# Transposes in visits of eight, two sub-blocks' transposes on VectorE, and the last output rows by two engines

## The chip, the cores and the metric

One core of a Trainium2 chip. The metric is the device time of one execution in microseconds. The kernel before takes 866.93 us in the median of three runs (866.83 to 867.17).

## What is computed

Three stages, one after the other, on 2304 tokens of width 512:

```python
scores = scale * np.matmul(q, k.transpose(0, 1, 3, 2))   # 4 batches, 8 heads, 576 tokens, 64 wide
mask = (rel >= 0) & (rel < 64)                           # a window of 64 tokens
attn = softmax(np.where(mask, scores, -1e9)); x = np.matmul(attn, v)
h = x @ w_in; x = np.maximum(h, 0) ** 2 @ w_out          # 512 -> 2048 -> 512
h = x @ w2_in; P = a0 + a1*h + a2*h2 + a3*h3
Q = 1 + abs(b0)*abs(h) + abs(b1)*h2; out = (P / (Q + 1e-6)) @ w2_out
```

Inputs and output are float32. Each large product is made of three float32r matmuls on high and low parts (high x high, high x low, low x high).

## The kernel before

The tokens are cut into five blocks of 512 (the last has 256), and into 18 sub-blocks of 128, numbered from 0. Attention is done by sub-block. Layer 1 (`l` = 0, the squared ReLU) runs over the blocks in order, layer 2 (`l` = 1, the rational function) after it over the blocks with the last two swapped. Within a block the 2048 hidden columns go by in 16 steps `j` of 128: `h_mm` (lines 776 to 803; matmuls on L788, L798) makes the hidden columns, `mid1` or `mid2` (L869, L911) applies the function and splits the result into high and low parts, and `out_mm` (L809; matmuls on L819 for layer 1, L821 for layer 2) adds the product into the four accumulators in PSUM. While block b of layer 1 runs, the attention of block b + 1 is done in slots that lie between its matmuls (`slots_of`, L969), and the weights are read and split on the way by `convert` (L422): in block 0 those of layer 1, needed at once (last operation L458, tiles `wih`, `wil`, `wo`), in blocks 1 to 3 those of layer 2, which go back to DRAM.

A sub-block `i` has these slots. `slot_q` and `slot_k` (L503, L522) turn its queries and keys: four TensorE transposes each (L515, L538) into a PSUM bank, then a copy by ScalarE or VectorE. From sub-block `NPE` = 10 on they are not turned on TensorE: `squares` (L351) copies queries and keys within DRAM, in pieces of 32 floats, into an order from which VectorE's transpose of 32 x 32 squares (L507, L529) does the rest. The scores (`slot_s`, matmuls on L621) go into two banks; `softmax` (L630) follows on VectorE and ScalarE. `slot_p` (L688) turns the probabilities, twice per sub-block, by four TensorE transposes (L699) and a copy (L704); from sub-block `NPD` = 8 on they are written to DRAM and read back in four pieces by POOL's DMA queue (L684, L685) and turned by VectorE (L692). `slot_x` (L728) makes the values (L708) and `split_x` their high and low parts. For sub-blocks after the block's first and below NPD, `slot_sx` puts the scores of `i` and the values of `i - 1` into one visit of TensorE. Outside the first block the PSUM banks for transposes and scores are `t0` and `t1`.

The order of the work is found when the kernel is built. `Plan.add` (L58) collects items, each with the engines that could do it, a cost in ns, the buffers that it reads and writes and a due time; `Plan.run` (L91) takes again and again the item that can start first, the more urgent of equals, and so fixes each engine's order, and that of SP's DMA queue ("dma"). The hardware then follows that order with semaphores. Slots are spread over 0.9 of a block's planned span (L1020 to L1024). The squares copies are listed from L1004 on: the item of step 9 + 2c + y (c the pair of heads, y keys or queries) of batch 2, and 17 + 2c + y of batch 3, each waiting for that step's low part from `mid1`. One item is four DMAs of SP.

The last block of layer 2 ends with accumulator 3. Its last matmuls are split into two halves of 256 columns (L826 to L833), and `evac2` (L946) copies each half out (L956) and stores it by SP (L957); all other rows are copied and stored whole (L962, L963).

```python
179      NPE = sum(n for _, n in blocks[:2]) // 128 + 2
...
973      o += ([("sx", i)] if first < i < NPD else [("s", i), ("x", i - 1)] if i > first else [("s", i)])
...
1008     sq_list.append((9 + 2 * c + y if z < B - 1 else 17 + 2 * c + y, x, c, z))
```

Of the kernel before, what the change touches and what calls it, by code (L numbers as in the profile page):

```python
# [47 lines left out]
class Plan:  # L48
# [9 lines left out]
    def add(self, engines, emit, reads=(), writes=(), due=None):  # L58
        it = Item(engines, emit, due)
        for b in reads:  # L60
            assert b.writers and not b.over
            for w in b.writers:
                it.deps[w] = True
        for b in writes:
            assert not b.over
            if not b.writers:
                for p in b.prev:
                    for w in p.writers + p.readers:
                        it.deps[w] = True
            for w in b.writers + b.readers:  # L70
                it.deps[w] = True
        for b in reads:
            b.readers.append(it)
        for b in writes:
            b.writers.append(it)
        it.deps.pop(it, None)
        for d in it.deps:
            d.users.append(it)
        self.items.append(it)
        return it  # L80

# [63 lines left out]
def window_attention__moe_relu2__moe_rational_kernel(  # L145
# [355 lines left out]
    qT, kT, sm, pT = {}, {}, {}, {}  # L501

    def slot_q(i, due):  # L503
        src = nat["q", i]
        if i >= NPE:
            t = qT[i] = buf(QTP, [128, HP, 128])
            plan.add({"dve": dve(512)}, lambda e: V.transpose(  # L507
                t.t.rearrange("p c t -> p (c t)"), src.t.rearrange("p h d -> p (h d)")), [src], [t], due)
            return
        ps = ps_buf()  # L510

        def tr(_):
            s = src.t.rearrange("p h d -> p (h d)")
            for c in range(HP):
                T.transpose(ps.t[:, c, :], s[:, c * 128:(c + 1) * 128], ident)  # L515

        plan.add({"pe": 430}, tr, [src], [ps], due).slack = rest(i)
        t = qT[i] = buf(QTP, [128, HP, 128])
        plan.add({"act": act(512, True), "dve": dve(512)}, lambda e: (
            A.copy(out=t.t, in_=ps.t) if e == "act" else V.tensor_copy(t.t, ps.t)), [ps], [t])  # L520

    def slot_k(i, due):  # L522
# [16 lines left out]

        plan.add({"pe": 430}, tr, [src], [ps], due).slack = rest(i)  # L540
        if i < NS0:
# [146 lines left out]
    def slot_p(i, n, due):  # L688
# [11 lines left out]

        plan.add({"pe": 430}, tr, [src] + [f for _, f in [own[i]] if n] if i in own else [src], [ps], due).slack = rest(i)
        t = pT[i, n] = early(NF - 5 - i, 2 + n, 128) if i < NS0 else buf(PT, [128, 4, 128])
# [53 lines left out]
    def split_x(i, ps):  # L756
# [3 lines left out]
        if bi == 0 and 2 * o == blocks[0][1]:  # L760
# [8 lines left out]

    fns = {"y": slot_y, "K": lambda z, due: slot_half("k", z, due), "Q": lambda z, due: slot_half("q", z, due),  # L770
           "S": slot_S, "q": slot_q, "k": slot_k, "s": slot_s, "sx": slot_sx, "p": slot_p, "x": slot_x}


# [32 lines left out]

    ends = []

    def out_mm(l, bi, j, g, due):  # L809
        n = blocks[bi][1]  # L810
        gh, gl = g
        wh, wl = wt[l, j, 1]

        def mm(m, cs=slice(0, KT)):
            for z, (w, y) in enumerate(((wh, gh), (wh, gl), (wl, gh)) if l == 0 else
                                       ((wh, gh), (wl, gh), (wh, gl))):
                st, en = (j == 0 and z == 0), (j == NF - 1 and z == 2 and cs.stop == KT)
                if l == 0:
                    T.matmul(out=v4(acc[l, bi, m].t, n), lhsT=w.t[:, m, :], rhs=y.t[:, :n // 128, :], start=st, stop=en)  # L819
                else:  # L820
                    T.matmul(out=v4(acc[l, bi, m].t, DM)[:, cs], lhsT=y.t[:, m, :], rhs=w.t[:, cs], start=st, stop=en)  # L821

        for m in range(KT if l == 0 else n // 128):
            if j == 0:
                acc[l, bi, m] = buf(f"acc{m}", [128, 512], F32, psum)
            if l and bi == orders[1][-1]:  # L826
                if j == NF - 1 and m == n // 128 - 1:
                    ends.extend(halves(acc[l, bi, m]))
                    for z, b in enumerate(ends):
                        b.prev = []  # L830
                        plan.add({"pe": 3 * MM[256]}, lambda e, m=m, z=z: mm(m, slice(2 * z, 2 * z + 2)),
                                 [wh, wl, gh, gl, acc[l, bi, m]], [b], due + z)
                    continue  # L833
            plan.add({"pe": 3 * MM[n if l == 0 else 512]}, lambda e, m=m: mm(m), [wh, wl, gh, gl], [acc[l, bi, m]],
                     due + m)
# [110 lines left out]
    def evac2(bi):  # L946
        t0, n = blocks[bi]
        for m in range(n // 128):
            due = finish - (n // 128 - 1 - m) * 1400 if bi == orders[1][-1] else finish
            if due == finish and ends:  # L950
                c = acc[1, bi, m]
                for z, b in enumerate(ends):
                    o = buf(LD, [128, H, D], view=lambda t: t.rearrange("p h d -> p (h d)")[:, 0:256])
                    cs = slice(z * 256, z * 256 + 256)
                    plan.add({"act": act(256, True), "dve": dve(256)}, lambda e, cs=cs, o=o: (
                        A.copy(out=o.t, in_=c.t[:, cs]) if e == "act" else V.tensor_copy(o.t, c.t[:, cs])), [b], [o])  # L956
                    plan.add({"dma": 364}, lambda e, o=o, m=m, cs=cs: nc.sync.dma_start(  # L957
                        out=out[t0 + m * 128:t0 + (m + 1) * 128, cs], in_=o.t), [o], due=due)
                continue
            c, o = acc[1, bi, m], buf(LD, [128, H, D], view=lambda t: t.rearrange("p h d -> p (h d)"))  # L960
            plan.add({"act": act(DM, True), "dve": dve(DM)}, lambda e, c=c, o=o: (
                A.copy(out=o.t, in_=c.t) if e == "act" else V.tensor_copy(o.t, c.t)), [c], [o])  # L962
            plan.add({"dma": 728}, lambda e, o=o, m=m: nc.sync.dma_start(  # L963
                out=out[t0 + m * 128:t0 + (m + 1) * 128, :], in_=o.t), [o], due=due)

# [3 lines left out]
    def slots_of(first, last):  # L969

        o = []
        for i in range(first, last):
# [121 lines left out]
```

## Time and profile before

| what | value |
|---|---|
| median of three runs | 866.93 us (866.83 to 867.17) |
| the profiled execution: its time, its span | 866.46 us, 864.5 us |
| TensorE matmuls (PE) | 856.6 us busy, 99% of the span |
| weight loads (PEld) | 717.2 us, 83% |
| VectorE (DVE) | 644.1 us, 74% |
| ScalarE (ACT) | 548.4 us, 63% |
| GpSimd (POOL) | 66.6 us, 8% |
| granted TensorE clock | 1.00, which is 2.4 GHz |

The span is what the profiler saw of the program; the rest of the execution's own time, 2.0 us, lies around it. Busy times are shares of the whole span, while the stages have different limits: layer 1 with the attention beside it goes on to about 380 us, layer 2 follows. Matmuls are pipelined: one begins before the last has ended, so the times that count are those from start to start. In the timelines, several like instructions that follow one another stand as one line, with their count at its end.

### The profile page before, as it was taken

How to read it: one execution, taken by the hardware profiler on the slowest of the kernel's cores; microseconds unless marked ns; L12 is line 12 of the kernel's file. 1: busy time of each engine (PE TensorE's matmuls, PEld its weight loads, DVE VectorE, ACT ScalarE, POOL GpSimd, SP SyncE). 2: the span in 40 equal slices, each digit the busy share in tenths (PEclk: the TensorE clock that was granted, in tenths of full speed). 3: DMA queues.
4: the chain of work that ended last, by engine and by line, in shares of the span. 5: the costliest groups of instructions: out<-in, count | busy, mean ns of one | idle time of the engine just before them, and what ended most of it. 6: DMA issues, size and time to landing. Idle time of an engine off the chain costs nothing.

```text
span 864.5 us, 14326 instructions
## 1 busy us (share of the span) xinstructions
PE 856.6 (99%) x5195; PEld 717.2 (83%) x5195; DVE 644.1 (74%) x1388; ACT 548.4 (63%) x1153; POOL 66.6 (8%) x124
## 2 busy tenths in 40 slices
PE   8999999999999999999999999999999999999998
PEld 7888888888888888888999888888888888988886
DVE  6999855666576656444313999999999999989994
ACT  7888755556554555554445766666666666878773
POOL 3000002222022221120000000000000000000000
PEclk9999999999999999999999999999999999999999
DMA  9977966999587776643499900300020003000001
GB/s 192 277 226 226 240 142 171 277 256 292 162 291 218 215 239 216 223 146 122 174 329 328 314 1 2 132 15 0 1 80 19 0 1 122 26 1 25 0 1 50
DMA packets 159831, 124.29 MB, mean 144 GB/s; under 512 B 94864, under 2 KB 136080, under 8 KB 157712
## 3 DMA queue, kind: packets, MB, share of 16 engines
q1 hardware_dynamic: 155600, 112.88, 44.5%
q0 software_dynamic: 4160, 10.49, 4.1%
q8 instruction: 41, 0.67, 0.3%
q14 instruction: 30, 0.25, 0.1%
HBM read 87.17 MB, written 40.37 MB: 148 GB/s over the span
## 4 chain that ended last, share of the span: by engine, by line
PE 98%; DVE 2%; ACT 0%; issue 0%; POOL 0%; ACTq 0%; POOLq 0%; DVEq 0%
PE h L798 34%; PE acc L819 23%; PE acc L821 23%; PE t L798 11%; PE t L621 2%; PE t L708 1%; PE t L699 0%; PE h L708 0%; DVE wih L655 0%; PE acc L984 0%; PE t L515 0%; PE acc L708 0%; DVE wil L655 0%; PE t L627 0%; PE h L788 0%; DVE wo L704 0%
## 5 line engine op out<-in xcount | busy, mean ns | idle before, releaser
L819 PE MATMUL acc<-g,wo 128*128 128x512 f32 (+1 forms) x960 | 214.5, 371 | 0.0
L819 PEld LDWEIGHTS acc<-g,wo 128*128 128x128 f32 x960 | 167.1, 189 | 30.6 <-issue 0.5
L798 PE MATMUL h<-xh,wih 128*128 128x512 f32 (+1 forms) x476 | 177.4, 373 | 0.0
L798 PE MATMUL h<-xl,wih 128*128 128x512 f32 (+1 forms) x476 | 175.3, 368 | 0.0
L798 PE MATMUL h<-xh,wil 128*128 128x512 f32 (+1 forms) x476 | 175.2, 368 | 0.0
L881 DVE TENSOR_TENSOR g<-cvr,g 128x512 fp32r<-128x512 f32 (+1 forms) x80 | 50.8, 635 | 98.5 <-ACT cvr L879 98.4
L874 ACT ACTIVATE cvr<-h 128x512 f32<-128x512 f32 (+1 forms) x80 | 44.2, 553 | 113.6 <-PE h L798 108.7
L798 PEld LDWEIGHTS h<-xh,wih 128*128 128x128 f32 x476 | 89.7, 189 | 16.0 <-issue 1.2
L798 PEld LDWEIGHTS h<-xh,wil 128*128 128x128 f32 x476 | 89.8, 189 | 15.2
L798 PEld LDWEIGHTS h<-xl,wih 128*128 128x128 f32 x476 | 89.8, 189 | 14.3
L821 PE MATMUL acc<-wo,cvr 128*128 128x512 f32 (+1 forms) x387 | 93.6, 388 | 0.0
L821 PE MATMUL acc<-wo,g 128*128 128x512 f32 x384 | 93.1, 390 | 0.0
L821 PEld LDWEIGHTS acc<-wo,cvr 128*128 128x128 f32 x387 | 71.8, 188 | 14.4
L821 PEld LDWEIGHTS acc<-wo,g 128*128 128x128 f32 x384 | 71.6, 188 | 14.5
L925 DVE SCALAR_TENSOR_TENSOR kT<-kT,b,sm 128x512 f32<-128x512 f32 (+1 forms) x80 | 55.7, 696 | 16.1 <-ACT kT L920 13.3
L927 ACT ACTIVATE raw<-kT,cb 128x512 f32<-128x512 f32 (+1 forms) x80 | 54.9, 686 | 8.8 <-DVE kT L925 5.5
L798 PE MATMUL t<-xl,wih 128*128 128x512 f32 (+1 forms) x160 | 58.9, 368 | 0.0
L798 PE MATMUL t<-xh,wil 128*128 128x512 f32 (+1 forms) x160 | 58.9, 368 | 0.0
L798 PE MATMUL t<-xh,wih 128*128 128x512 f32 (+1 forms) x160 | 58.8, 368 | 0.0
L659 ACT ACTIVATE sm<-sm,nm 128x128 f32<-128x128 f32 x112 | 43.8, 393 | 22.3 <-DVE nm L655 22.0
L938 DVE SCALAR_TENSOR_TENSOR pT<-pT,coef,raw 128x512 f32<-128x512 f32 (+1 forms) x80 | 55.7, 696 | 1.7
L921 ACT ACTIVATE sm<-h,coef 128x512 f32<-128x512 f32 (+1 forms) x40 | 25.8, 646 | 47.5 <-PE h L798 47.5
(176 smaller groups left out, 1356.5 us busy)
## 6 DMA issues: line engine op xcount, KB each, us to landing
raw<-in_moe_w_in_dram SPq DMA_DIRECT2D x60, 256.0 KB, 4.2
raw<-in_moe_w_out_dram SPq DMA_DIRECT2D x30, 512.0 KB, 4.6
w2h_d<-raw SPq DMA_DIRECT2D x32, 256.0 KB, 3.5
w2l_d<-cvr SPq DMA_DIRECT2D x32, 256.0 KB, 3.7
ld<-in_v_dram SPq DMA_DIRECT2D x25, 256.0 KB, 4.5
p_d<-sm POOLq DMA_DIRECT2D x20, 256.0 KB, 3.9
sm<-p_d POOLq DMA_DIRECT2D x80, 64.0 KB, 4.6
out_dram<-ld SPq DMA_DIRECT2D x17, 256.0 KB, 2.1
```

The source lines that it names most:

```text
L621: T.matmul(out=ps[gl].t[o:o + 64, hp, :], lhsT=qt.t[r, hp, gl * W:(gl + 1) * W], rhs=kt.t[r, hp, -W - 128:][:, :128] if not gl else kt.t[r ...
L659: A.activation(out=head(c), in_=head(c), func=ACTF.Exp, scale=-1.0, bias=nm.t[:, c:c + 1], accum_out=su.t[:, c:c + 1])
L708: T.matmul(out=ps.t[e * 64:(e + 1) * 64, hp, gl * W:(gl + 1) * W], lhsT=v.t[rows, 2 * hp + e, :], rhs=(pT[i, gl].t[:, (e ^ gl) * 2:(e ^ gl ...
L798: T.matmul(out=v4(hp.t, n), lhsT=w.t[:, (c ^ 2) * 128:((c ^ 2) + 1) * 128], rhs=x.t[:, :n // 128, c, :], start=(c == 0 and z == 0), stop=( ...
L819: T.matmul(out=v4(acc[l, bi, m].t, n), lhsT=w.t[:, m, :], rhs=y.t[:, :n // 128, :], start=st, stop=en)
L821: T.matmul(out=v4(acc[l, bi, m].t, DM)[:, cs], lhsT=y.t[:, m, :], rhs=w.t[:, cs], start=st, stop=en)
L874: plan.add({"act": act(n, True)}, lambda e: A.activation(out=r.t[:, :n], in_=hp.t[:, :n], func=ACTF.Relu), [hp], [r])
L881: plan.add({"dve": dve(n)}, lambda e: V.tensor_tensor(out=gl.t[:, :nq], in0=v4(r.t, n), in1=gh.t[:, :nq].bitcast(F32), op=ALU.subtract), [ ...
L921: plan.add({"act": act(n, True, 1)}, lambda e: A.activation(out=f(ab), in_=f(hb), func=ACTF.Abs, scale=coef[:, 4:5]), [hb, coef_b], [ab])
L925: plan.add({"dve": dve(n, ptr=1)}, lambda e: V.scalar_tensor_tensor(out=f(h2), in0=f(h2), scalar=b1, in1=f(ab), op0=ALU.mult, op1=ALU.add) ...
L927: plan.add({"act": act(n, ptr=1)}, lambda e: A.activation(out=f(y), in_=f(h2), func=ACTF.Ln, scale=2.0 ** -63, bias=cb[:, 0:1]), [h2], [y])
L938: plan.add({"dve": dve(n, ptr=1)}, lambda e: V.scalar_tensor_tensor(out=f(u), in0=f(u), scalar=coef[:, 0:1], in1=f(y), op0=ALU.subtract, o ...
```

## The change

The constants become NPE = 9 and NPD = 7: sub-block 9's queries and keys and sub-block 7's probabilities are turned by VectorE. The squares of batch 2 are copied five steps earlier. In the slots, `paired` joins a sub-block's query and key transposes into one item of TensorE with eight transposes, and likewise its two probability transposes; the joined item stands where the query's slot stood, or the second probability's. In the blocks concerned these are queries and keys of sub-blocks 6, 7 and 8 and probabilities of 5 and 6. The last matmuls are no longer split; the two halves of the last 128 rows are copied by ScalarE and VectorE, and stored by ScalarE's and SP's queues.

```diff
-    NPE = sum(n for _, n in blocks[:2]) // 128 + 2
-    NPD = sum(n for _, n in blocks[:2]) // 128
+    NPE = sum(n for _, n in blocks[:2]) // 128 + 1
+    NPD = sum(n for _, n in blocks[:2]) // 128 - 1
...
+    joint = []
+
+    def visit(reads, ps, tr, due, i):
+
+        if joint and joint[0]:
+            it, fs = joint.pop()
+            fs.append(tr)
+            plan.link(it, reads, [ps])
+            return
+        fs = [tr]
+        it = plan.add({"pe": 860 if joint else 430}, lambda e: [f(e) for f in fs], reads, [ps], due)
+        it.slack = rest(i)
+        if joint:
+            joint[0] = it, fs
+
+    def slot_qk(i, due):
+        joint.append(None)
+        slot_q(i, due)
+        slot_k(i, due)
+
+    def slot_pp(i, due):
+        joint.append(None)
+        slot_p(i, 0, due)
+        slot_p(i, 1, due)
...
-        plan.add({"pe": 430}, tr, [src], [ps], due).slack = rest(i)
+        visit([src], ps, tr, due, i)
...
-        def mm(m, cs=slice(0, KT)):
+        def mm(m):
...
-            if l and bi == orders[1][-1]:
-                if j == NF - 1 and m == n // 128 - 1:
-                    ends.extend(halves(acc[l, bi, m]))
...
+            if bi == orders[1][-1] and due == finish:
+                for z, e in enumerate(("act", "dve")):
+                    cs = slice(z * DM // 2, (z + 1) * DM // 2)
+                    o = buf(LD, [128, H, D], view=lambda t: t.rearrange("p h d -> p (h d)")[:, :DM // 2])
+                    plan.add({e: 334}, lambda e, o=o, c=c, cs=cs: (
+                        A.copy(out=o.t, in_=c.t[:, cs]) if e == "act" else V.tensor_copy(o.t, c.t[:, cs])), [c], [o])
+                    plan.add({"dma": 364}, lambda _, o=o, e=e, cs=cs, rows=rows: (A if e == "act" else nc.sync).dma_start(
+                        out=rows[:, cs], in_=o.t), [o], due=due)
                 continue
...
+    def paired(slots, first):
+
+        o = []
+        for x, d in slots:
+            kind, i = x[:2]
+            if kind in "qk" and first < i < NPE:
+                o += [(("qk", i), d)] if kind == "q" else []
+            elif kind == "p" and first <= i < NPD:
+                o += [(("pp", i), d)] if x[2] else []
+            else:
+                o.append((x, d))
+        return o
...
-                sq_list.append((9 + 2 * c + y if z < B - 1 else 17 + 2 * c + y, x, c, z))
+                sq_list.append((4 + 2 * c + y if z < B - 1 else 17 + 2 * c + y, x, c, z))
...
-                    slots = [(x, start[0, bi] + per * y) for y, x in enumerate(slots)]
+                    slots = paired([(x, start[0, bi] + per * y) for y, x in enumerate(slots)], f + 1)
```

## Rows read from the trace of the kernel before

**Rows 1.** The page's chain that ended last, shares of the span by engine.

```profile
PE 98%; DVE 2%; ACT 0%; issue 0%; POOL 0%; ACTq 0%; POOLq 0%; DVEq 0%
```

**Rows 2.** Windows: busy us of each engine (instructions), clock, DMA share, GB/s.

```profile
core 0: us, PE busy (x) PEld busy (x) DVE busy (x) ACT busy (x) POOL busy (x), PEclk, DMA share, GB/s
...
60.00:93.00 33.00, 33.00 (x215) 27.25 (x214) 30.74 (x74) 26.80 (x64) 0.00 (x0) 1.00 0.80 228
93.00:126.00 33.00, 33.00 (x235) 27.05 (x234) 25.09 (x62) 21.35 (x49) 0.00 (x0) 1.00 0.84 194
```

**Rows 3.** Timeline of TensorE, 95.9 to 102.6: start, us, engine, line, instruction, count.

```profile
95.91 1.15 PE L708 MATMUL h<-pT,ld 128*64 128x64 f32 x32
97.00 3.02 PE L819 MATMUL acc<-g,wo 128*128 128x512 f32 x12
99.86 0.39 PE L798 MATMUL h<-xh,wih 128*128 128x512 f32 x1
...
102.58 0.39 PE L819 MATMUL acc<-g,wo 128*128 128x512 f32 x1
```

**Rows 4.** Timeline of TensorE around sub-block 7's probabilities and values, 106.2 to 122.1.

```profile
106.20 0.39 PE L798 MATMUL h<-xh,wil 128*128 128x512 f32 x1
106.44 0.60 PE L699 MATMUL t<-ident,sm 128*128 128x128 f32 x4
...
108.95 0.27 PE L538 MATMUL t<-ident,ld 128*128 128x128 f32 x1
...
114.66 0.39 PE L798 MATMUL h<-xh,wil 128*128 128x512 f32 x1
...
115.24 2.99 PE L819 MATMUL acc<-g,wo 128*128 128x512 f32 x12
118.06 0.39 PE L798 MATMUL h<-xh,wih 128*128 128x512 f32 x1
...
118.83 1.15 PE L708 MATMUL t<-pT,ld 128*64 128x64 f32 x32
...
122.09 0.39 PE L819 MATMUL acc<-g,wo 128*128 128x512 f32 x1
```

**Rows 5.** Timeline of TensorE around two visits side by side, 81.8 to 85.7.

```profile
81.84 0.39 PE L798 MATMUL h<-xh,wil 128*128 128x512 f32 x1
82.07 0.60 PE L515 MATMUL t<-ident,ld 128*128 128x128 f32 x4
82.50 0.60 PE L699 MATMUL t<-ident,sm 128*128 128x128 f32 x4
82.86 2.98 PE L819 MATMUL acc<-g,wo 128*128 128x512 f32 x12
85.68 0.39 PE L798 MATMUL h<-xh,wih 128*128 128x512 f32 x1
```

**Rows 6.** Timelines of VectorE and TensorE: sub-block 8's round trip, block 1's start.

```profile
155.41 0.70 DVE L692 STREAM_TRANSPOSE pT<-sm 128x512 f32<-128x512 f32 x1
...
130.25 0.39 PE L798 MATMUL h<-xh,wih 128*128 128x512 f32 x1
...
132.38 1.10 PE L621 MATMUL t<-kT,qT 64*64 64x128 f32 x32
```

**Rows 7.** Squares of keys (ns min/median/max, first and last start); the eighth group's weights.

```profile
L325 SPq DMA_DIRECT2D k_squares_d<-in_k_dram x32: 562/626/1770, 93.1 to 186.0; - x32
...
68.85 0.69 DVE L458 TENSOR_TENSOR wil<-cvr,wih 128x512 fp32r<-128x512 f32 x1
...
71.56 0.39 PE L798 MATMUL h<-xh,wih 128*128 128x512 f32 x1
```

**Rows 8.** The last rows: ScalarE's copies; SP's issues (ns) and their landing.

```profile
860.83 0.65 ACT L956 COPY ld<-acc 128x256 f32<-128x256 f32 x2 [1.48 <-PE acc L821]
...
L957 SPq DMA_DIRECT2D out_dram<-ld x2: 332/352/371, 861.2 to 861.7; - x2
...
DMA to landing us min/median/max: 1.7/1.8/1.8
```

More of the change, by code (lines that the diff above doesn't have):

```diff
@@ L59, in add, with link @@
         it = Item(engines, emit, due)
+        self.link(it, reads, writes)
+        self.items.append(it)
+        return it
+    @staticmethod
+    def link(it, reads, writes):
         for b in reads:
@@ L77, in add @@
         for d in it.deps:
-            d.users.append(it)
-        self.items.append(it)
-        return it
+            if it not in d.users:
+                d.users.append(it)
     @staticmethod
@@ L538, in tr @@
                 T.transpose(ps.t[:, c, :], s[:, c * 128:(c + 1) * 128], ident)
-        plan.add({"pe": 430}, tr, [src], [ps], due).slack = rest(i)
+        visit([src], ps, tr, due, i)
         if i < NS0:
@@ L699, in tr @@
                 T.transpose(ps.t[:, c, :], src.t[:, c, :], ident)
-        plan.add({"pe": 430}, tr, [src] + [f for _, f in [own[i]] if n] if i in own else [src], [ps], due).slack = rest(i)
+        visit([src] + [f for _, f in [own[i]] if n] if i in own else [src], ps, tr, due, i)
         t = pT[i, n] = early(NF - 5 - i, 2 + n, 128) if i < NS0 else buf(PT, [128, 4, 128])
@@ L805, in window_attention__moe_relu2__moe_rational_kernel @@
     HPS_ring = (("h0", "h1"), ("h0", "t0", "h1", "t1"))
-    ends = []
     def out_mm(l, bi, j, g, due):
@@ L812, in out_mm @@
         wh, wl = wt[l, j, 1]
-        def mm(m, cs=slice(0, KT)):
+        def mm(m):
             for z, (w, y) in enumerate(((wh, gh), (wh, gl), (wl, gh)) if l == 0 else
                                        ((wh, gh), (wl, gh), (wh, gl))):
-                st, en = (j == 0 and z == 0), (j == NF - 1 and z == 2 and cs.stop == KT)
+                st, en = (j == 0 and z == 0), (j == NF - 1 and z == 2)
                 if l == 0:
@@ L820, in mm @@
                 else:
-                    T.matmul(out=v4(acc[l, bi, m].t, DM)[:, cs], lhsT=y.t[:, m, :], rhs=w.t[:, cs], start=st, stop=en)
+                    T.matmul(out=v4(acc[l, bi, m].t, DM), lhsT=y.t[:, m, :], rhs=w.t, start=st, stop=en)
         for m in range(KT if l == 0 else n // 128):
@@ L825, in out_mm @@
                 acc[l, bi, m] = buf(f"acc{m}", [128, 512], F32, psum)
-            if l and bi == orders[1][-1]:
-                if j == NF - 1 and m == n // 128 - 1:
-                    ends.extend(halves(acc[l, bi, m]))
[L829 to L833, printed above, removed]
             plan.add({"pe": 3 * MM[n if l == 0 else 512]}, lambda e, m=m: mm(m), [wh, wl, gh, gl], [acc[l, bi, m]],
@@ L948, in evac2 @@
         for m in range(n // 128):
+            c = acc[1, bi, m]
             due = finish - (n // 128 - 1 - m) * 1400 if bi == orders[1][-1] else finish
[L950 to L958, printed above, removed]
+            rows = out[t0 + m * 128:t0 + (m + 1) * 128, :]
+            if bi == orders[1][-1] and due == finish:
[6 more added lines that the diff above has]
+                        out=rows[:, cs], in_=o.t), [o], due=due)
                 continue
-            c, o = acc[1, bi, m], buf(LD, [128, H, D], view=lambda t: t.rearrange("p h d -> p (h d)"))
+            o = buf(LD, [128, H, D], view=lambda t: t.rearrange("p h d -> p (h d)"))
             plan.add({"act": act(DM, True), "dve": dve(DM)}, lambda e, c=c, o=o: (
                 A.copy(out=o.t, in_=c.t) if e == "act" else V.tensor_copy(o.t, c.t)), [c], [o])
-            plan.add({"dma": 728}, lambda e, o=o, m=m: nc.sync.dma_start(
-                out=out[t0 + m * 128:t0 + (m + 1) * 128, :], in_=o.t), [o], due=due)
+            plan.add({"dma": 728}, lambda e, o=o, rows=rows: nc.sync.dma_start(out=rows, in_=o.t), [o], due=due)
     coef_b, na_b, b1_b = (Buf(plan, x, lambda: None) for x in ("coef", "na", "b1"))
```

2 lines of the change are left out of this document (1 added, 1 removed).

## The prediction

> **What bounds the kernel now.** I read the chain of waits first: 98% of it is TensorE [rows 1], so nothing shortens the run unless it takes work off TensorE, fills a gap of it, or shortens what follows its last matmul. The windows say the same for the stretch that the change touches: from 60 to 126 us TensorE is busy all the time, at granted clock 1.00 [rows 2]. There is thus no wait to remove; the change has to be priced by TensorE's own work. The same windows show what could take the cover away: VectorE is busy for 30.74 of 33 us between 60 and 93 us, the DMA engines for 0.80 and 0.84 of the two stretches, and POOL not at all in either [rows 2]. VectorE and the DMA queue are nearly full just where more work arrives.
>
> How TensorE's work is priced: not by the busy time of a matmul (it is pipelined, so busy times overlap) but from start to start. Twelve 512-column matmuls go from 99.86 to 102.58 us, 0.227 us each [rows 3]. A stretch with a visit costs what it takes beyond that.
>
> **Transposes taken off TensorE.** The eighth sub-block's two probability visits (four transposes each) and the tenth's query and key visits go. From the matmul before one visit (106.20) to the start of the next visit (108.95) stand ten matmuls, 2.27 us by the cadence, in 2.75 us: the visit costs 0.48. The other probability visit: 114.66 to 118.06 holds thirteen, 2.95 us of 3.40: 0.45 [rows 4]. The two visits of the tenth sub-block are the same four transposes of 128x128 between the same kind of matmuls, so I take 0.45 to 0.48 for each, and 4 x 0.47 = 1.88 us for the four.
>
> **Visits of eight.** Five pairs are joined: queries and keys of sub-blocks 6, 7 and 8, probabilities of 5 and 6. One such pair stands side by side already: from 81.84 to 85.68 are thirteen matmuls and eight transposes, 3.84 - 2.95 = 0.89 us [rows 5], against two at 0.47. So a join saves 0.05. Of the ten visits that are joined, eight stand alone now and two are that pair: 8 x 0.47 + 0.89 = 4.65 against 5 x 0.89 = 4.45, a gain of 0.20 us. Bounds: nothing, if the planner had put the visits side by side anyway, to 0.4 us, if they had all cost 0.48 and saved the whole exit seen in the pair.
>
> **The visit that comes apart.** With NPD at 7 the scores of sub-block 7 no longer share a visit with the values of sub-block 6 ("sx"); they become two visits. Values in the joint visit take 97.00 - 95.91 = 1.09 us [rows 3]. Values alone: 118.06 to 122.09 holds twelve matmuls, 2.72 us, so 4.03 - 2.72 = 1.31 [rows 4]. A visit of its own costs 0.22 us more; lost.
>
> **Work that moves to other engines.** VectorE gets four block transposes of 0.70 us [rows 6] and loses up to four copies out of PSUM of like size that either it or ScalarE did. I cost this at nothing: the cover is TensorE's row of matmuls, and the two probability transposes fall after 93 us, where VectorE has 33 - 25.09 = 7.9 us free in 33 [rows 2]. Without that cover it would cost 2 x 0.70 = 1.4 us. POOL issues two more writes of the probabilities and eight more reads; it has nothing else to do between 93 and 126 us [rows 2], and nobody else waits in its queue there. What can be late is the chain behind them: scores, softmax, write, four reads, transpose, values. The ninth sub-block shows it: scores at 132.38, second transpose finished at 155.41 + 0.70 = 156.1, so 23.7 us [rows 6]. The eighth's scores now stand in the joint visit just ahead of 95.91 [rows 3], so its values would be possible at about 119, which is where they are now (118.83, [rows 4]); the block that needs them starts at 130.25 [rows 6]. 11 us of slack: cost nothing.
>
> The copies into squares of queries and keys begin five steps earlier, and the eight items of batch 2 carry 576 tokens each instead of 448. One squares item is four DMA issues on SP of 0.626 us [rows 7], 2.5 us in which the loads of weights queue behind. A step of block 0 lasts (130.25 - 71.56)/9 = 6.5 us ([rows 6, 7]: the eighth column group's first matmul is at 71.56, the next block's at 130.25), so the first item moves from 93.1 to about 60 us. The eighth group's weights are ready at 68.85 + 0.69 = 69.54 and first used at 71.56 [rows 7]: 2.0 us of slack against 2.5 us of issue, if the item stands ahead of their load in the queue. I take nothing, as each load also waits for a raw buffer, in which an item can slip; the bounds are 0 and 0.5 us for one item, and the first rival below for several.
>
> **The last rows.** Now two copies of 256 columns run on ScalarE, one after the other: both start after TensorE's last matmul (860.83, 0.65 us together), so the split of the last matmuls into halves let nothing start early. SP issues the halves at 861.2 and 861.7, each landing 1.8 us later [rows 8]. After the change the second copy runs beside the first on VectorE and its issue beside the other's. Best case: both issued by 861.28 (a VectorE copy of some 0.42 us, an estimate: half of the 0.70 that it takes for 512 columns [rows 6], and a fixed part), landing at 863.1 instead of 863.5: 0.4 us. Worst: an issue on ScalarE's queue, which this trace has nowhere, could lose what is won, and cost 0.1 beyond. I take 0.25, nearer the best end, because the second copy's 0.3 us leaves the chain whatever the issue costs. The Trainium skill (DMA: Bandwidth & Descriptors, Issuing engines are not separate DMA queues) speaks against the second half of it: DMAs of two engines share the same sixteen DMA engines, and only issue time is saved. By that rule the two halves would share bandwidth; the term would then be about 0.1 us and the sum 1.96 instead of 2.11. No row before has two engines storing at once.
>
> **Sum.** 1.88 + 0.20 - 0.22 + 0.25 = 2.11 us less. The profiled execution took 866.46 us (span 864.5), and becomes 864.35; it stands 0.47 under the median of 866.93, which becomes 864.8. What a measurement of this kernel can tell from no change is about 0.2%, 1.73 us, so the forecast lies only 0.4 us beyond it.
>
> **Rivals.**
> (a) Slower: squares in front of weights. For it: the DMA engines' share rises from 0.80 to 0.84 as the squares begin while the rate falls from 228 to 194 GB/s [rows 2], so they are costly transfers; margin at the eighth group is 2.0 us; VectorE has only 2.3 us free in 33 to catch up. Against it: the squares ran from 93 us on beside the last weights, and TensorE was busy all of those 33 us. Price: three of the eight items unrecovered, 3 x 2.5 - 2.0 = 5.5 us of idle TensorE before the matmuls of the eighth to eleventh groups, so 864.8 + 5.5 = 870.3. It decides from 3.8 us of such idle time on, where the gain of 2.11 is used up and 1.73 more. Chance 0.11. The Trainium skill (DMA: Bandwidth & Descriptors, Specifications) asks for pieces of at least 512 bytes for line rate, and the squares go in pieces of 32 floats; the fall in rate agrees.
> (b) Half the gain lost, within 0.2%. A visit of eight starts when the later of its two inputs is there and both banks of the pair are free; TensorE takes its work in order, so whatever is late stands as idle time, with the matmuls queued behind it. Three key transposes come two slots earlier than now, behind an SP queue that has the squares in it; and the weights of one group may be 0.5 us late. One wait of a squares item less its slack, 0.5 us, in two places gives 865.8. For it: the small slack above. Against it: TensorE never idled beside the same visits. Chance 0.28.
> (c) The eighth sub-block's round trip ends over 11 us later than the ninth's did: the block's first matmuls wait. 5 us too late would give 869.8. The DMA share is high there too, but 11 us would have to be lost first. Chance 0.02, counted with slower.
>
> **Numbers.** Forecast case 0.59, (b) 0.28, (a) and (c) 0.13. The forecast's own range is 864.2 (join and tail at their best, 0.4 and 0.4: 2.46, and run scatter) to 865.2. Leaving out most of (a) and (c), the range reaches to 867.0, where (b) ends. Faster by over 0.2%: 0.59; within: 0.28; slower: 0.13.
>
> **What would show it.** Right: four visits fewer and one more on TensorE, 0.89 us for each visit of eight, TensorE busy without a gap from 60 to 126 us, ScalarE's and VectorE's last copies side by side. Wrong: idle TensorE before a first matmul of a column group, or before a visit of eight, in the first 130 us; the next block starting later than 130.25 less what was saved; or a last store that lands no earlier than 2.7 us after the last matmul.

## The result, and the profile after

The changed kernel takes 872.72 us in the median of five runs (871.17 to 872.99), against 866.93 us before: 1.0061 times as long, with a 95% interval of 1.005 to 1.0072. It is slower by 5.8 us, where 2.1 us less were forecast, and outside the range that was given. The profiled execution took 871.42 us, its span is 869.6 us. One of the eleven executions of e5 below took 2938 us and is left out of its ratio.

The chain of waits of the changed kernel is no longer TensorE alone; loads of weights and SP's issues are in it [rows 1]:

```profile
PE 94%; SPq 2%; DMA 2%; DVE 1%; issue 1%; ACT 1%; DVEq 0%; ACTq 0%
```

The windows name the place. From 93 to 126 us TensorE is busy for 28.86 us of 33, and the mean granted clock is 0.95; in the stretch before, the DMA engines went from 0.80 to 0.92 [rows 2]. These are two rows of one answer, and two of another whose stretches are all 66 us and the slow one alone:

```profile
60.00:93.00 33.00, 33.00 (x213) 27.36 (x211) 27.91 (x70) 23.24 (x53) 0.00 (x0) 1.00 0.92 217
93.00:126.00 33.00, 28.86 (x178) 22.89 (x178) 24.34 (x60) 20.77 (x47) 5.72 (x10) 0.95 0.94 250
...
60.00:126.00 66.00, 61.86 (x389) 50.24 (x389) 52.26 (x129) 44.00 (x100) 5.72 (x10) 0.97 0.93 233
99.80:103.10 3.30, 3.06 (x35) 2.78 (x36) 3.19 (x16) 2.71 (x11) 0.00 (x0) 0.50 0.59 181
```

The timeline of TensorE shows one long wait, before the values of sub-block 6 (the lines of the changed kernel have other numbers: L738 is L708 of before, L828 is L798, L847 is L819, L685 is L655, and in `convert` L448 is L443 and L463 is L458):

```profile
95.60 0.39 PE L828 MATMUL h<-xh,wil 128*128 128x512 f32 x1
100.04 1.98 PE L738 MATMUL t<-pT,ld 128*64 128x64 f32 x32 [4.05 <-issue]
101.95 0.80 PE L847 MATMUL acc<-g,wo 128*128 128x512 f32 x1
```

It idles for 4.05 us, and then works for some 3.3 us at a granted clock of 0.50, the lower level of 1.2 GHz; the row of 99.8 to 103.1 above is that stretch. "Issue" says only that no event of the profile ended the wait. What ended it is found by going to the engine that had to free a bank. The scores of sub-block 7 have just filled both banks `t0` and `t1`, and the values want `t0` too. VectorE's timeline:

```profile
93.54 0.68 DVE L463 TENSOR_TENSOR wo<-cvr,wo 128x512 fp32r<-128x512 f32 x1
96.54 0.43 DVE L448 TENSOR_SCALAR raw<-raw 128x512 uint32<-128x512 uint32 x1 [2.31 <-DMA raw<-in_moe_w_in_dram]
...
98.67 0.43 DVE L448 TENSOR_SCALAR raw<-raw 128x512 uint32<-128x512 uint32 x1 [0.75 <-DMA raw<-in_moe_w_in_dram]
99.02 0.28 DVE L685 CUSTOM_DVE_ANT_0 sm<-t,mask 128x128 f32<-128x128 f32 x1
...
99.65 0.29 DVE L685 CUSTOM_DVE_ANT_0 sm<-t,mask 128x128 f32<-128x128 f32 x1
```

VectorE stands still for 2.31 and 0.75 us until weights have landed. The first pass of the softmax (L685) is queued behind; four of its instructions free the bank, the last ends at 99.65 + 0.29 = 99.94, and TensorE starts at 100.04. That it was the bank is read from the code and the times, and e4 below bears it out. Why were the weights late? SP's timeline:

```profile
88.30 2.95 SPq L330 DMA_DIRECT2D k_squares_d<-in_k_dram  x4
91.36 2.09 SPq L330 DMA_DIRECT2D raw<-in_moe_w_in_dram  x4
93.55 0.41 SPq L330 DMA_DIRECT2D raw<-in_moe_w_out_dram  x1
94.00 4.19 SPq L330 DMA_DIRECT2D q_squares_d<-in_q_dram  x4
98.29 1.56 SPq L330 DMA_DIRECT2D raw<-in_moe_w_out_dram  x1
```

A squares item of four issues stands in front of the loads, and takes 2.95 and 4.19 us, not 2.5: single issues are held up. In the view of the squares' own tile one issue of queries or keys takes up to 3.2 or 3.5 us, against 1.4 or 1.77 before in the same stretch. An item of before had gone beyond 2.5 us already:

```profile
98.78 3.38 SPq L325 DMA_DIRECT2D q_squares_d<-in_q_dram  x4
```

All issues of SP between 60 and 126 us, summed from the traces, take 52.4 us in the changed kernel and 39.0 before. Loads of weights also take longer from issue to landing: 5.1 us in the median of the input weights between 60 and 126 us, 3.9 before. The view of waits between 60 and 126 us adds up what the two engines that split the weights lose by it:

```profile
ACT cvr L446 <- DMA raw<-in_moe_w_in_dram: 8.7, 6, 4.4
DVE raw L448 <- DMA raw<-in_moe_w_in_dram: 7.9, 7, 2.3
...
ACT cvr L446 <- DMA raw<-in_moe_w_out_dram: 4.0, 4, 1.9
...
DVE raw L448 <- DMA raw<-in_moe_w_out_dram: 2.3, 1, 2.3
```

22.9 us together; before, the same view has 1.4. The eighth group of columns, which had 2.0 us of slack, gets its weights at 72.81 + 0.68 = 73.49 us, 0.07 us before its first matmul (a row of VectorE's timeline and one of TensorE's):

```profile
72.81 0.68 DVE L463 TENSOR_TENSOR wil<-cvr,wih 128x512 fp32r<-128x512 f32 x1
...
73.56 0.50 PE L828 MATMUL h<-xh,wih 128*128 128x512 f32 x1
```

Two smaller waits follow. The values of sub-block 7 begin and stop again, until VectorE has turned the second half of the probabilities:

```profile
125.91 0.34 PE L738 MATMUL t<-pT,ld 128*64 128x64 f32 x4
127.00 1.04 PE L738 MATMUL t<-pT,ld 128*64 128x64 f32 x28 [0.76 <-DVE pT L722]
```

And the two engines at the end do not work side by side (L977 is L956, L978 is L957):

```profile
865.88 0.37 ACT L977 COPY ld<-acc 128x256 f32<-128x256 f32 x1 [0.77 <-PE acc L849]
866.28 0.37 ACTq L978 DMA_DIRECT2D out_dram<-ld  x1
866.29 0.42 DVE L977 COPY ld<-acc 128x256 f32<-128x256 f32 x1 [8.20 <-ACT ld L977]
866.74 0.33 SPq L978 DMA_DIRECT2D out_dram<-ld  x1
```

VectorE's copy starts when ScalarE's has ended (865.88 + 0.37 = 866.25). The second store is issued 0.86 us after the first copy began; before it was 861.7 - 860.83 = 0.87 [rows 8]. Nothing is won.

The visits themselves are as forecast. From 57.78 to 61.62 are thirteen matmuls, 2.95 us, and eight transposes: 3.84 - 2.95 = 0.89 us, the same as side by side before [rows 5]:

```profile
57.78 1.07 PE L847 MATMUL acc<-g,wo 128*128 128x512 f32 x4
58.69 0.60 PE L545 MATMUL t<-ident,ld 128*128 128x128 f32 x4
59.12 0.60 PE L568 MATMUL t<-ident,ld 128*128 128x128 f32 x4
59.48 0.48 PE L828 MATMUL h<-xh,wih 128*128 128x512 f32 x1
...
61.62 0.39 PE L828 MATMUL h<-xh,wih 128*128 128x512 f32 x1
```

The parts add up. From the matmul at 33.2 us to the end of layer 1 (its last matmul before ends at 470.16 us, not at about 380; only the attention ends earlier) the changed kernel takes 5.1 us more in its trace. TensorE is idle for 4.90 us more (4.05, 0.76 and 0.09), the slow clock costs some 1.7 us (an estimate: half of the time that the clock was at 0.50), and TensorE's own work is 1.5 us shorter, where the prediction's sum, without the last rows, has 1.86. From block 1's first matmul on, where only sub-block 9's two visits are gone, the rest of layer 1 takes 338.94 us against 339.91, 0.97 less, where the sum has 0.94. That matmul stands at 130.25 us before [rows 6], and here at

```profile
136.30 0.39 PE L828 MATMUL h<-xh,wih 128*128 128x512 f32 x1
```

### The profile page after: what moved, and what is told of

Same layout as the page of the kernel before. It is cut to its first block, busy times and chain, and to the rows that moved or that the text cites. A ratio compares the mean times of both kernels' runs of the same rounds, so it can differ in the third digit from the quotient of the medians.

```text
span 869.6 us, 14319 instructions
## 1 busy us (share of the span) xinstructions
PE 856.6 (99%) x5176; PEld 715.9 (82%) x5176; DVE 652.2 (75%) x1401; ACT 542.7 (62%) x1140; POOL 72.3 (8%) x134
## 4 chain that ended last, share of the span: by engine, by line
PE 94%; SPq 2%; DMA 2%; DVE 1%; issue 1%; ACT 1%; DVEq 0%; ACTq 0%
PE h L828 33%; PE acc L849 23%; PE acc L847 22%; PE t L828 11%; SPq L330 2%; PE t L738 2%; PE t L651 2%; DMA raw<-in_moe_w_in_dram 1%; DMA ld<-in_k_dram 1%; DMA raw<-in_moe_w_out_dram 0%; PE h L818 0%; PE acc L738 0%; PE t L729 0%; PE h L738 0%; PE t L545 0%
## 5 line engine op out<-in xcount | busy, mean ns | idle before, releaser
L847 PE MATMUL acc<-g,wo 128*128 128x512 f32 (+1 forms) x960 | 214.6, 371 | 0.0
L847 PEld LDWEIGHTS acc<-g,wo 128*128 128x128 f32 x960 | 167.8, 189 | 31.1 <-issue 0.7
L828 PE MATMUL h<-xh,wih 128*128 128x512 f32 (+1 forms) x476 | 177.2, 372 | 0.0
L828 PE MATMUL h<-xh,wil 128*128 128x512 f32 (+1 forms) x476 | 175.3, 368 | 0.1
L828 PE MATMUL h<-xl,wih 128*128 128x512 f32 (+1 forms) x476 | 175.2, 368 | 0.0
L828 PEld LDWEIGHTS h<-xh,wih 128*128 128x128 f32 x476 | 89.7, 188 | 16.4 <-issue 1.2
L828 PEld LDWEIGHTS h<-xh,wil 128*128 128x128 f32 x476 | 89.7, 189 | 15.5 <-DVE wil L463 0.5
L828 PEld LDWEIGHTS h<-xl,wih 128*128 128x128 f32 x476 | 89.7, 189 | 14.4
L849 PE MATMUL acc<-wo,cvr 128*128 128x512 f32 x384 | 93.6, 390 | 0.0
L828 PE MATMUL t<-xl,wih 128*128 128x512 f32 (+1 forms) x160 | 58.9, 368 | 0.0
L828 PE MATMUL t<-xh,wil 128*128 128x512 f32 (+1 forms) x160 | 58.8, 368 | 0.0
L828 PE MATMUL t<-xh,wih 128*128 128x512 f32 (+1 forms) x160 | 58.8, 367 | 0.0
L949 ACT ACTIVATE raw<-raw,cb 128x512 f32<-128x512 f32 (+1 forms) x80 | 54.5, 681 | 1.6
```

Of the source, the lines that this page charges most:

```text
L828: T.matmul(out=v4(hp.t, n), lhsT=w.t[:, (c ^ 2) * 128:((c ^ 2) + 1) * 128], rhs=x.t[:, :n // 128, c, :], start=(c == 0 and z == 0), stop=( ...
L849: T.matmul(out=v4(acc[l, bi, m].t, DM), lhsT=y.t[:, m, :], rhs=w.t, start=st, stop=en)
L949: plan.add({"act": act(n, ptr=1)}, lambda e: A.activation(out=f(y), in_=f(y), func=ACTF.Exp, scale=-1.0, bias=cb[:, 1:2]), [y], [y])
```

## The experiments

Each run was timed against the kernel before on the same chip (medians of before from 866.82 to 867.22 us). "Waits" is the sum of the rows of VectorE and ScalarE waiting for loads of weights, from 60 to 126 us, as above; "TensorE" its busy time in those 66 us. An engine that is late itself waits less, so the first column alone does not say how late the weights are (see e15).

| run | waits, us | TensorE, us of 66 | median, us | ratio to before (95%) |
|---|---|---|---|---|
| before | 1.4 | 66.00 | 866.93 | |
| changed | 22.9 | 61.86 | 872.72 | 1.0061 (1.005 to 1.0072) |
| e1 visits of eight and tail | 5.5 | 66.00 | 866.46 | 0.9994 (0.9986 to 1.0003) |
| e2 NPD 7 alone | 7.4 | 65.19 | 867.72 | 1.0004 (0.9995 to 1.0012) |
| e3 NPE 9 and early squares alone | 18.2 | 64.79 | 868.11 | 1.0015 (1.0006 to 1.0024) |
| e4 changed, other bank | 28.5 | 62.15 | 871.97 | 1.0058 (1.0042 to 1.0074) |
| e5 changed, NPE 10 | 14.1 | 65.16 | 867.39 | 1.0007 (0.9998 to 1.0016) |
| e6 changed, NPD 8 | 20.9 | 63.21 | 869.34 | 1.0029 (1.0018 to 1.0041) |
| e7 changed, long pieces | 18.3 | 63.28 | 866.60 | 1.0000 (0.9992 to 1.0009) |
| e8 changed, squares from step 6 | 16.7 | 62.56 | 869.02 | 1.0024 (1.0014 to 1.0035) |
| e9 no early squares, joint visit, late read | 5.7 | 66.00 | 865.98 | 0.9988 (0.9979 to 0.9997) |
| e10 long pieces, joint visit | 11.1 | 65.43 | 866.38 | 0.9996 (0.9988 to 1.0005) |
| e11 changed, joint visit, late read | 22.6 | 62.34 | 870.94 | 1.0051 (1.0039 to 1.0064) |
| e12 early squares alone | 16.1 | 66.00 | 867.50 | 1.0008 (0.9999 to 1.0018) |
| e13 squares by POOL | 4.1 | 59.74 | 965.42 | 1.1122 (1.1102 to 1.1141) |
| e14 as e13, joint visit, late read | 2.6 | 65.67 | 964.59 | 1.112 (1.1098 to 1.1143) |
| e15 squares by ScalarE | 5.2 | 61.72 | 875.42 | 1.0096 (1.0083 to 1.011) |
| e16 as e15, joint visit, late read | 9.4 | 63.01 | 874.65 | 1.0081 (1.0068 to 1.0094) |

**One part at a time (e1, e2, e3).** Two theories stood at first: the bank that the split visit now shares (theory bank), or the squares ahead of the weights (theory squares).

e1 is the changed kernel with

```diff
-    NPE = sum(n for _, n in blocks[:2]) // 128 + 1
-    NPD = sum(n for _, n in blocks[:2]) // 128 - 1
+    NPE = sum(n for _, n in blocks[:2]) // 128 + 2
+    NPD = sum(n for _, n in blocks[:2]) // 128
-                sq_list.append((4 + 2 * c + y if ...
+                sq_list.append((9 + 2 * c + y if ...
```

> Only the visits of eight and the two engines at the end (NPE 10, NPD 8, squares at step 9 as before). If the loss comes from the bank or from the squares, both are absent here and the gain of both parts as read from the traces stays: about 0.2 us from the joins and 0.3 us from the tail, so 866.4 us. If a visit of eight by itself makes TensorE wait, 867 us or more, with idle time before a visit of eight.

866.46 us, with no idle TensorE: the visits of eight do no harm. The gain, 0.5 us beside its own runs of before (866.98), is not clear of noise. In the trace the stretch from the matmul at 33 us to the end of layer 1 is 0.28 us shorter, and what follows TensorE's last matmul is as long as before: the joins have their 0.20, the last rows nothing.

e2 is the kernel before with `// 128 - 1` in the line of NPD.

> The kernel before with NPD 7 alone: two probability visits less (0.93 us), one visit more (0.22 us). Theory bank (the values of sub-block 6 now need one of the two banks that the scores of sub-block 7 fill, and wait for VectorE): a wait before those values of 1 to 5 us, 867.5 to 871 us, though the squares stand where they were. Theory squares (the early copies stand before weight loads in SP's queue and VectorE stands still): no squares here, so no wait, 866.2 us. Theory both (the bank turns VectorE's standstill into TensorE's): the wait is under 1 us, 866.2 to 867 us.

No wait before the values of sub-block 6, though they share the bank there too; but one before those of 7:

```profile
120.31 0.51 PE L708 MATMUL t<-pT,ld 128*64 128x64 f32 x10 [0.81 <-DVE pT L692]
```

The ratio is that of no change: two visits saved, given back by the split and this wait.

e3 is the kernel before with `// 128 + 1` in the line of NPE and `4 + 2 * c` in that of the squares.

> The kernel before with NPE 9 and the squares five steps earlier, nothing else. Theory bank: no bank changes, 0.95 us gained, 866.0 us. Theory squares: VectorE waits for weights and TensorE idles 2 us or more between 60 and 130 us, 868 to 871 us. Theory both: VectorE waits for weights, but TensorE idles under 1 us, 866 to 867 us.

VectorE and ScalarE wait 18.2 us for weights, but TensorE idles little, 1.2 us before an `out_mm`. The time lies in the range of theory squares, the idle time between those of theory squares and theory both. The parts' ratios, -0.06%, 0.04% and 0.15%, add up to 0.13%; together they cost 0.61%.

**The bank (e4).** The changed kernel, with

```diff
+    def slot_xh(i, due):
+        ps = buf(HPS_ring[0], [128, 512], F32, psum, cols(128))
+        reads, writes, mm = slot_x(i, due, ps)
+        plan.add({"pe": 1250}, mm, reads, writes, due).slack = rest(i)
+        split_x(i, ps)
-        o += (... else [("s", i), ("x", i - 1)] if i > first ...
+        o += (... else [("s", i), ("xh" if i == NPD > first else "x", i - 1)] if i > first ...
```

> The changed kernel, but the values of sub-block 6 get a bank of the other ring (h0, h1), as they had in the joint visit. Theory bank and theory both: the wait of 4 us before these values is gone, with the slow clock behind it, and 5 us of time: 866 to 868 us. Theory squares: VectorE is as late as before, the wait moves to the next matmuls that need its results, 870 to 873 us.

The wait before the values is gone, and the time is not. TensorE now waits at the first matmuls of column groups (in e4 these lines are six higher: L834 is L828):

```profile
103.25 0.50 PE L834 MATMUL h<-xh,wih 128*128 128x512 f32 x1 [1.50 <-ACT cvr L900]
...
117.01 0.50 PE L834 MATMUL h<-xh,wih 128*128 128x512 f32 x1 [1.24 <-ACT wih L462]
```

The bank was the place where the lateness met TensorE, not its cause.

**One part undone at a time (e5, e6, e8).** e5 undoes the lines of NPE and of the squares, e6 that of NPD, e8 has `6 + 2 * c` in the squares' line.

> The changed kernel with NPE 10 and the squares at step 9 again; visits of eight, NPD 7 and the tail stay. Theory squares (the copies ahead of weight loads are what costs): the sum of the parts measured alone, 866.5 and 0.7 for the round trip, 867 us, no wait before the values of sub-block 6 though they still share the bank. Theory bank (the split visit costs by itself once visits are joined): a wait of 2 us or more before these values, 869 to 872 us.

867.39 us and no wait at the shared bank: theory squares. What is left is 0.84 us before the values of sub-block 7.

> The changed kernel with NPD 8: visits of eight, the tail, NPE 9 and the early squares stay. If the parts add up, 866.5 and 1.1 us: 867.6 us. If the early squares by themselves carry the loss once the visits are joined, 870 to 873 us, with weights late for the columns of steps 7, 10 and 13. If it takes the round trip's DMAs (1 MB more between 100 and 120 us) as well, the weights of step 13 come in time here and the time is under 868 us.

869.34 us, between the cases. So about half of the loss is there without sub-block 7, and its part adds the rest.

> The changed kernel with the squares from step 6 on instead of 4, the latest that the load of sub-block 9 allows but one. Theory squares: the weights of step 7 are in time again (slack 2 us, as before the change), those of steps 10 to 14 are not, and the time is between, 868 to 872 us. Theory bank: no change, 871 to 873 us.

869.02 us: two steps later, 3.7 us less.

**Pieces (e7, e10).** In e7 each squares DMA carries as many bytes, but in pieces of 2304 bytes and not 128, so that the queries and keys of the last sub-blocks are scrambled:

```diff
-                    yield (sq_d[nm][a * 32:(a + 1) * 32, c, o // 32:(o + n) // 32, :],
-                           src[bi, 2 * c + a // 2, s:s + n, a % 2 * 32:a % 2 * 32 + 32].rearrange(
-                               "(b j) i -> j b i", j=32))
+                    yield (sq_d[nm][a * 32:(a + 1) * 32, c, o // 32:(o + n) // 32, :].rearrange("j b i -> j (b i)"),
+                           src[bi, 2 * c + a // 2, s + a % 2 * (n // 2):s + a % 2 * (n // 2) + n // 2, :].rearrange(
+                               "(j x) d -> j (x d)", j=32))
```

> The changed kernel; each squares DMA moves as many bytes to the same place, but from a contiguous stretch in pieces of 2304 bytes instead of 128 (so queries and keys of the last sub-blocks are scrambled). As many DMAs stand ahead of the weight loads. Theory issue time (SP's 0.63 us for each issue is what delays the weights): unless the issues get shorter with the pieces, still 870 us or more. Theory small pieces (the DMA engines are held by the many pieces, and loads beside them land later): the weights are in time, 866 to 868 us.

866.60 us: 6.1 us of the changed kernel's time hang on the size of the pieces, with as many issues in front of the weights. The weights are not in time, though: the waits are 18.3 us, and TensorE idles 1.22 us before the values of sub-block 6 and 1.50 us before those of 7, with no slow clock. The rows of the squares in e7:

```profile
L330 SPq DMA_DIRECT2D q_squares_d<-in_q_dram x16: 489/588/590, 67.7 to 110.0; - x16
...
L330 SPq DMA_DIRECT2D k_squares_d<-in_k_dram x16: 494/588/3331, 60.2 to 102.3; - x16
```

and in the changed kernel:

```profile
L330 SPq DMA_DIRECT2D q_squares_d<-in_q_dram x16: 556/766/3197, 67.8 to 114.5; - x16
...
L330 SPq DMA_DIRECT2D k_squares_d<-in_k_dram x16: 557/633/3514, 60.2 to 106.1; - x16
```

Long pieces hardly shorten the quickest issue (489 against 556 ns), but fewer are held up: 3 of the 32 take over 1 us, against 8, and the 32 take 22.7 us together, against 31.4. The input weights' way from issue to landing is little shorter, 4.9 us in the median against 5.1. The Trainium skill (DMA: Bandwidth & Descriptors, Specifications) has line rate only from pieces of 512 bytes on. The traces agree: the DMA engines move 233 GB/s at a share of 0.93 in the changed kernel (the row of 60 to 126 us above), and 234 GB/s at 0.80 in e7:

```profile
60.00:126.00 66.00, 63.28 (x427) 51.72 (x427) 55.84 (x136) 46.70 (x104) 5.71 (x10) 1.00 0.80 234
```

e10 is e7 with the joint visit kept, `first < i < max(NPD, 8)` in the line that is 973 before.

> The changed kernel with squares in long pieces (scrambled data, as in e7) and the joint visit kept for sub-block 7. If the prediction's sum of TensorE work is right and only the small pieces and the shared bank break it: no wait of 1.4 us before the values of 6, and 1.9 us of transposes, 0.2 of joins gained, less about 1 us at the values of 7: 865.0 to 865.9 us. If the sum is wrong as well: 866.6 us as in e7.

866.38 us, above the range that the sum should have given: the wait before the values of 6 is gone; 0.57 us before those of 7 are left and 0.18 us later on. The profiled execution took 865.80 us, 0.66 less than before, where the sum has 1.88 + 0.20 less these 0.75 us of waits, 1.33. The other 0.7 us were not found.

**What sub-block 7 adds, and the squares alone (e11, e12).** e11 is the changed kernel with the joint visit kept and

```diff
-                 ...  reads=[b], own=2300, lag=5000)
+                 ...  reads=[b], own=2300, lag=5000 if i >= 8 else 9000)
```

> The changed kernel with the joint visit kept for sub-block 7 and 4 us more for its read back; the squares early and in small pieces. Theory: sub-block 7 adds to the loss of the early squares by its split visit and its read back only; then this is at the time without it (e6), 869.3 us or a little less. If its 1 MB of DMA traffic is what adds to that of the squares, 871 to 873 us.

870.94 us, between the two. It is 1.8 us under the changed kernel, which would be the split and the early read, but the two intervals overlap; 1.6 us more than e6 remain, and TensorE waits for the low parts that VectorE makes:

```profile
117.73 0.50 PE L847 MATMUL acc<-g,wo 128*128 128x512 f32 x1 [1.67 <-ACT g L896]
120.07 2.16 PE L847 MATMUL acc<-g,wo 128*128 128x512 f32 x6 [1.84 <-DVE g L901]
```

That fits the DMA traffic of the round trip, but no run took that traffic away alone.

e12 is the kernel before with `4 + 2 * c` alone.

> The kernel before with nothing but the squares of batch 2 from step 4 on. Theory small pieces: weights come late between steps 7 and 14 though no TensorE work has changed, and with no work taken off to set against it the loss is that of e3 and the 0.95 us that e3 gained: 868.5 to 870 us. If the squares need the other parts to do harm, 867 us as before.

A miss, as the time is no clear change: 16.1 us of waits for weights, and TensorE is busy for all of the 66 us. The lateness is there and nothing shows it but the waits of the two engines that split the weights:

```profile
60.00:126.00 66.00, 66.00 (x447) 54.09 (x446) 56.17 (x136) 48.72 (x112) 0.00 (x0) 1.00 0.87 219
```

**SP's queue or the DMA engines (e13 to e16).** To take the squares out of SP's queue, e13 issues them by POOL (`own=2600` in `squares`), e15 by ScalarE; e14 and e16 do the same with the joint visit and the late read.

> The changed kernel with the squares issued by POOL instead of SP: same bytes, same pieces of 128 bytes, same steps. Theory SP's queue (weight loads stand behind the squares' issues): the weights are in time, the time is near that of long pieces, 866 to 868 us. Theory DMA engines (their small pieces slow every load beside them): the loads land as late as in the changed kernel and the time stays at 870 us or more.

> As e13, with the joint visit kept for sub-block 7 and 4 us more for its read back. Theory SP's queue: no wait of TensorE over 0.5 us after 30 us, and all the transposes taken off count: e9's 866.0 less 0.95, 865.0 us. Theory DMA engines: as e11, 870 to 872 us.

965.42 and 964.59 us, 98 us lost, for a reason of its own: POOL issued a squares DMA every 2.7 to 5.9 us between 50 and 125 us,

```profile
POOL k_squares_d L330 <- issue: 95.4, 31, 6.1
```

3.1 us of idle time ahead of each, and the probabilities' own DMAs stood behind them. Up to 119 us the weights were nearly in time (4.1 us of waits), but the squares did not stand at the same steps: POOL began them at 26.6 us, and issued 14 of them between 60 and 119 us, where SP issues all 32 in the changed kernel. So the two theories were not told apart.

> The changed kernel with the squares issued by ScalarE. Theory SP's queue: the weights are in time as far as ScalarE's own work on them allows (20 us of issues in all on an engine that has some 10 us free between 60 and 93), 866 to 869 us. Theory DMA engines: loads land 1 us later than before the change, as in the changed kernel, and the time is 870 us or more.

> As e15 with the joint visit kept for sub-block 7 and its late read back. Theory SP's queue: 865 to 868 us, under e11's 870.9 by 3 us or more. Theory DMA engines: 870 to 872 us, as e11.

875.42 and 874.65 us, slower still, so "866 to 869" was wrong. The waits for loads fell to 5.2 us with the small pieces on the DMA engines at the same steps, and the input weights took 4.4 us from issue to landing. But ScalarE, which splits the weights, is now late itself, held up by its own issues:

```profile
ACT wo L462 <- DMA k_squares_d<-in_k_dram: 4.4, 1, 4.4
ACT wih L462 <- DMA k_squares_d<-in_k_dram: 3.2, 1, 3.2
```

So the weights are not in time here either. Set beside the same load of the kernel before, the 27 loads of weights that it issues between 60 and 126 us land 5.8 us later on average, 5.5 of it at the issue already, though no squares stand in SP's queue; that a late ScalarE frees the raw buffers late would explain it. The small waits of e15 thus decide nothing between the theories.

The same comparison of the other traces says more. In the changed kernel the loads land 6.7 us later, of which 5.8 are there when SP issues them; in e7 4.4, of which 3.5. What is added on the way is 0.9 us in both. SP's issues between 60 and 126 us take 52.4 us in the one and 41.6 in the other. Long pieces thus bring the loads out of SP's queue sooner and not faster over the engines, as theory SP's queue has it; that the issues are held up because small pieces keep the DMA engines busier is likely, and not shown. A load also goes out late when its raw buffer comes free late, as in e15, so how much of the 5.8 us began in the queue stays open.

**A version that beats both (e9).** Visits of eight, NPD 7 and the tail, with NPE 10 and the squares where they were, the joint visit and the late read.

> Visits of eight, the tail and NPD 7, with NPE 10 and the squares at step 9; the scores of sub-block 7 keep their joint visit with the values of 6, and the planner is told 4 us more for the read back of sub-block 7's probabilities. If the 0.83 us before the values of 7 was a round trip that the planner had put too early, it is gone, and with 0.93 us of transposes and 0.2 of joins less the time is 865.7 us. If the DMA engines are simply too busy there, the wait stays: 866.5 us or more.

865.98 us, 0.9988 times the time before (0.9979 to 0.9997). TensorE never idles:

```profile
60.00:93.00 33.00, 33.00 (x215) 27.49 (x214) 30.44 (x75) 26.64 (x60) 0.00 (x0) 1.00 0.81 235
93.00:126.00 33.00, 33.00 (x231) 27.15 (x230) 25.33 (x61) 21.88 (x50) 5.70 (x10) 1.00 0.88 206
```

The wait at the values of sub-block 7 was thus a read back that the planner had put too early, and 4 us more in its table mend it (e10, which has the joint visit and long early squares but not the late read, still has 0.57 us of it). The gain in the median is 0.84 us, where the sum has 0.93 + 0.20 for these parts. In the traces, from the matmul at 33.2 us (33.8 here) to the end of layer 1, it is 1.21 us: 435.73 against 436.94. The time up to that matmul differs by up to 0.9 us from one profiled execution to another.

## Why the prediction was wrong

- **The squares, taken at nothing.** This is the step that failed. The text priced one item, 2.5 us of issue against 2.0 us of slack, and took zero since an item could slip in while loads wait for a raw buffer. The runs show 22.9 us of waits for weights in its place, and behind them 4.05 us of idle TensorE and a slow clock. Without the early squares (and with NPE 10) the time is 867.39 us (e5), with them in long pieces 866.60 (e7). Eight items come, at a step each; issues are held up beyond their 0.626 us, which is a median, and the same row had 1.77; and the slack is one for all. Rival (a) had the mechanism, with a chance of 0.11, and its price of 870.3 was 2.4 us short. Its place was another: the idle time came before the values of sub-block 6, and in e4, where these values have a bank of their own, before first matmuls of column groups. Its counter-argument, that the squares had run beside the last weights without harm, compared unlike stretches: in the kernel before, the groups of columns that begin from 99.86 us on had their weights 4.6 to 8.8 us ahead, the eighth had 2.0 us. The row of DMA share and rate was read, and should have carried more weight.
- **The visit that comes apart, 0.22 us.** The work was right: scores and values take 2.35 us beyond the cadence in the joint visit, 2.57 apart in e2. The bank was missed: in the joint visit the values had a bank of the other ring, alone they stand behind the scores of sub-block 7 in `t0`. As long as VectorE is in time that costs nothing (e2, e5); in the changed kernel it turned VectorE's standstill into 4.05 us of idle TensorE and a slow clock after it.
- **The round trip, taken at nothing with 11 us of slack.** The slack was counted to the next block's start. But TensorE's order is fixed when the kernel is built: the values stand where the planner expected them, and TensorE waits there with everything behind it, 0.76 us here, 0.81 in e2. By the prediction's own numbers these values were possible at about 119 us and stood at 118.83: at that place there was no slack. Rival (c) looked at the wrong end, too.
- **The last rows, 0.25 us.** Nothing: both copies read one bank, and the second waited for the first. The Trainium skill (PSUM — Partial Sum Buffer, PSUM bank collisions raise a hardware error) states that engines must not access one bank of a partition at the same time, and that kernels guard it by semaphores. The rows agree, 866.29 after 866.25. It may be why the halves before also began only after the last matmul; no run shows that. The prediction weighed a page on DMA there and not this one.
- **Transposes taken off and visits of eight, 1.88 and 0.20 us.** A visit of eight costs 0.89 us as read. The traces have the parts, each where TensorE is never idle: 0.28 us for the joins (e1), 1.21 for the joins and the two probability visits (e9; 1.13 in the sum), 0.97 for sub-block 9's visits (0.94). The whole 1.88 was never seen in one run free of waits.
- **The sum itself.** Costs were added as if independent. Weights that come late cost TensorE nothing as long as the splitting engines catch up: 16.1 us of waits with TensorE busy throughout (e12), 18.2 with 1.2 us idle (e3), 22.9 with 4.1 (changed). The order is not strict (e7 and e8 idle 2.7 and 3.4 us at 18.3 and 16.7), as it depends on where a late engine meets TensorE.

## What to carry to other kernels

Work moved off the busiest engine is paid in the queues that it goes through: count the DMAs that come with it, find what stands behind them, and sum their delay over all items against the one slack that they share. Look at the waits of the engines in between, not at the bound engine's idle time, to see how much of that slack is gone, and at when their inputs land, as an engine that is late itself waits less. And where an order is fixed beforehand, a late input costs at the place where its user stands in the order, not at the moment where its result is needed; a bank that two visits share is such a place.

## What the runs showed of the hardware that was not expected

- An issue on SP takes 0.56 us for 576 pieces of 128 bytes at the least, and up to 3.5 us in the busy stretch of the changed kernel.
- POOL issued the same DMA only every 2.7 to 5.9 us, in e13, while SP and ScalarE took 0.6 us; the kernel took 98 us longer.
- With the squares in pieces of 128 bytes the DMA engines' share was 0.93 from 60 to 126 us, in pieces of 2304 bytes 0.80, at 233 and 234 GB/s.
- After 4.05 us of idle TensorE its granted clock was at the lower level from 99.8 to 103.1 us.
